# One reciprocal per tile pair, all first-batch gathers on SyncE, and first-batch loads spread over the steps

## The chip, the cores and the metric

The kernel runs on one NeuronCore of a Trainium2 chip. The metric is the device time of one execution in microseconds (us), lower is better. Three runs of the kernel before the change gave 615.82, 616.46 and 617.23 us; the median is 616.46 us. One execution, the one of 617.23 us, was recorded with a hardware profile.

## The reference, cut to what matters

"Talking heads" attention, in which the heads are mixed before and after the softmax, and then a feed-forward network with a squared ReLU:

```python
scores = scale * np.matmul(q, k.transpose(0, 1, 3, 2))      # 8 batches, 12 heads, 448 x 448, head_dim 64
scores = np.einsum('bhij,hg->bgij', scores, w_pre)          # heads mixed
attn = np.exp(scores - max); attn = attn / (sum + 1e-09)    # softmax over j
attn = np.einsum('bhij,hg->bgij', attn, w_post)             # heads mixed again
x = np.matmul(attn, v) -> (3584, 768)
h = np.maximum(x @ w_in, 0.0)                               # w_in 768 x 2048
out = (h * h) @ w_out                                       # w_out 2048 x 768
```

## The kernel before, in words

Each batch is cut into 45 tiles of 10 queries. A tile holds its 10 queries times 12 heads on partitions, so that one matmul with a small block matrix (`pre`) mixes the heads. Two tiles make one step; there are 180 steps `ds` (and two more to drain), 22.5 for each batch. The steps run through these stages:

- `load_qk`, `load_v`, `load_w1`, `load_w2` issue DMAs from GpSimd (POOL). They convert float32 in HBM to bf16 in SBUF. For each batch there are six loads of q and k and three of v; the two weight matrices take eight loads each, once.
- `turn_unit` transposes q and k on TensorE (`tr_ps`), six units for each batch. `TURN` says at which step each unit runs; for batch 1 these are steps 15, 15, 16, 16, 17, 17.
- `score_pair` makes the scores of two heads for a block of 128 queries (`s_ps`); ScalarE (ACT) and VectorE (DVE) each cast one of the two to bf16 into the tile `S` (line 312). A batch has four blocks and there are only two `S` buffers, so the casts of a block wait until every gather from the block two before has landed.
- `gather` copies one tile's rows from `S` to a tile `G` with one DMA of 105 KB from SBUF to SBUF (line 329). There are `AHEAD + 2` = 12 `G` buffers, so a gather can be issued as soon as the `mix` of 12 tiles earlier has been done. At the start tiles 0 to 11 are gathered in one go.
- `mix(k)`, for the two tiles of step `k`, mixes the heads into two PSUM banks (`m_ps`, line 338). For each of them ACT takes the exponential with a row sum (`e_sb`, line 343), DVE the reciprocal of the sum (`rc`, line 345), and POOL scales and shifts (`d`, line 347).
- `unmix(k)`, two steps later (`LAG = 2`), mixes with `w_post` on TensorE (`at_ps`, line 369), and DVE casts into `at` (line 374).
- `av_unit` multiplies with v (`ot_ps`, line 185), ACT writes `xt` (line 196). `ffn1_unit` (`h_ps`, line 234) and `ffn2_unit` (`o_ps`, line 267) are the feed-forward network; they are put into a list of fillers and handed out over the steps by weight.

The order of TensorE and POOL is the order in which the program is written (`manual_schedule`); a planner orders DVE, ACT and SyncE (SP). `at_load(i, f, ...)` puts a load into POOL's order ahead of the work of tile `i`, that is, of step `i // 2`; the list for -1 is issued before step 0. DMAs of SP and ACT share eight completion semaphores in the order of the program, and each DMA waits until the one issued eight before it has landed.

In the kernel before, the gathers of batch 0 go in turn to SP and ACT:

```python
eng = nc.scalar if b == 0 and k % 2 else nc.sync
```

Of the kernel before, what the change touches and what calls it, by code (L numbers as in the profile page):

```python
# [9 lines left out]
F32 = mybir.dt.float32  # L10
ACT = mybir.ActivationFunctionType
# [3 lines left out]
B, H, S, D = 8, 12, 448, 64  # L15
# [18 lines left out]
OFF = 64 - H * (IQ // 2)  # L34
SCALE = 1.0 / 8.0
# [7 lines left out]
def kernel(  # L43
# [11 lines left out]
    nc = tc.nc  # L55
    P = nc.NUM_PARTITIONS
# [4 lines left out]
    work = ctx.enter_context(tc.tile_pool(name="work", bufs=1))  # L61
# [4 lines left out]
    def bank(name, dtype=F32):  # L66
        return psp.tile([P, 512 if dtype == F32 else 1024], dtype, name=name, tag="ps")
# [29 lines left out]
    def stripes(name, p0s):  # L97
        t = consts.tile([P, HQ], F32, name=name)
        for p0, c0 in zip((0, 64), p0s):
# [9 lines left out]
                            in0=stripe_pre[:, :].unsqueeze(2).to_broadcast([P, HQ, H]),  # L109
# [14 lines left out]

    gts = [work.tile([P, S], BF16, name=f"G{x}") for x in range(AHEAD + 2)]
    for t in gts:
        nc.vector.memset(t[0:OFF, :], 0.0)

    attn = [atp.tile([P, R, H, TW], BF16, name=f"at{x}") for x in range(2)]
    for t in attn:  # L130
# [166 lines left out]
    Sb, Gs, dsb = {}, {}, {}  # L297
# [16 lines left out]
    def queries(t, y):  # L314
        return max(0, min(HQ, S - IQ * t - HQ * y))
# [5 lines left out]
    def gather(k):  # L321

        b, t = steps[k]
        blk, tl = divmod(t, TPB)
        n = min(IQ, S - IQ * t)
        x = BLK_OFF[blk] + IQ * tl
        g = gts[k % len(gts)]
        eng = nc.scalar if b == 0 and k % 2 else nc.sync
        eng.dma_start(out=g[OFF:OFF + H * n, :], in_=Sb[(b, blk)][x:x + n, :, :])
        Gs[k] = g  # L330

    def mix(k):
        pss = [bank("m_ps") for _ in range(2)]
        gs = [Gs.pop(2 * k + x) for x in range(2)]
        for y in range(2):
            for x in range(2):
                rows = slice(64 * y, 64 * y + H * queries(steps[2 * k + x][1], y) if y else 64)
                nc.tensor.matmul(pss[y][64 * x:64 * x + 64, 0:S], lhsT=pre[rows, :], rhs=gs[x][rows, :],  # L338
                                 start=True, stop=True)
        for y in range(2):  # L340
            e = work.tile([P, S], F32, name="e_sb", tag="E", bufs=3)
            sm = work.tile([P, 1], F32, name="sm", tag="sm", bufs=4)
            nc.scalar.activation(out=e[:, :], in_=pss[y][:, 0:S], func=ACT.Exp, scale=SCALE, accum_out=sm[:, 0:1])  # L343
            rc = work.tile([P, 1], F32, name="rc", tag="rc", bufs=4)
            nc.vector.reciprocal(out=rc[:, :], in_=sm[:, :])  # L345
            d = dts[(2 * k + y) % ND]
            nc.gpsimd.tensor_scalar(out=d[:, 0:S], in0=e[:, :], scalar1=rc[:, 0:1], scalar2=-1.0 / S,  # L347
                                    op0=ALU.mult, op1=ALU.add)
            dsb[(k, y)] = d

# [43 lines left out]
    with tc.manual_schedule(engines={PE, POOL}):  # L394
# [10 lines left out]
        def at_load(i, f, *args):  # L405
            loads.setdefault(i, []).append(lambda: f(*args))

        for x in range(2):
            at_load(-1, load_w1, x)
        for x in range(3):  # L410
            at_load(-1, load_v, 0, x)
            at_load(44 + x, load_v, 1, x)
        for x in range(2, 8):
            at_load(-1, load_w1, x)
        for x in range(8):
            at_load(18 + 2 * x, load_w2, x)
        for x in range(6):
            at_load(6 + 2 * x, load_qk, 1, x)
            at_load(46 + 2 * x, load_qk, 2, x)
        for b in range(1, B):  # L420
            if b + 2 < B:
# [27 lines left out]
        def gathers_for(ds):  # L449
            while gathered[0] < min(2 * ds + AHEAD + 2, len(steps)):  # L450
                if issued[0] < needs(steps[gathered[0]]):
                    break
                gather(gathered[0])
                gathered[0] += 1
# [6 lines left out]
        for ds in range(nd + LAG):  # L461
# [37 lines left out]
            if now2:  # L499
                mix(ds)  # L500
# [37 lines left out]
```

The softmax here doesn't subtract the row's maximum and nothing guards it: scores larger than these inputs give would overflow.

## Time and profile before

| what | value |
|---|---|
| median of three runs | 616.46 us |
| the profiled execution, its own time | 617.23 us |
| its span, first to last instruction | 615.4 us |
| mean granted TensorE clock | 0.964 |
| busy: PE, DVE, POOL, ACT | 90%, 71%, 65%, 64% |
| gathers from SP / from ACT | 338 / 22 |
| reciprocals on DVE | 360, 154 ns each |

The busy shares are means over stages with different limits. The page cuts the span into 40 slices of 15.4 us each and gives a digit for each engine and slice. TensorE is at 9 in nearly every slice from the 12th on. It is between 4 and 8 in the first eight. The chain of waits names, for each stretch of time, the work that the end of the program hung on. Windows of the span give busy time for each engine in a stretch. A wait is put down to the engine whose semaphore came last.

### The profile page before, as it was taken

The page shows a single profiled execution, that of the slowest core. Times are in us where ns is not written, and L with a number is a line of the kernel's source. Part 1 is how long each engine was busy: PE and PEld are TensorE (multiplying, and loading weights), DVE is VectorE, ACT ScalarE, POOL GpSimd, SP SyncE. Part 2 cuts the span into 40 slices and gives each one's busy share as a digit, 9 for nine tenths or more (in the row PEclk, how much of TensorE's full clock was granted, in tenths as well). Part 3 has the DMA queues.
Part 4 walks back from the last instruction along what each step waited for, and adds up shares of the span by engine and source line. Part 5 has one row for each costly group of instructions (what it writes and reads, how often), then busy time and mean ns, then how long its engine had stood idle before and what let it go on. Part 6 is the DMA issues. An engine that isn't in the chain of part 4 may idle for free.

```text
span 615.4 us, 26843 instructions
## 1 busy us (share of the span) xinstructions
PE 556.6 (90%) x11154; PEld 313.2 (51%) x11154; DVE 434.4 (71%) x1123; ACT 396.1 (64%) x1196; POOL 397.8 (65%) x579
## 2 busy tenths in 40 slices
PE   5456888799799999999999899999999999999997
PEld 3124556554455456545555456545555455555554
DVE  5364999988687778876886768776887787755101
ACT  3364677556678866787578755786678767972320
POOL 7264838657459963898458944798458945892450
PEclk9655999999899999999999999999999999999999
DMA  9989958859645885488545875478543565431102
GB/s 141 227 169 160 199 99 148 149 84 176 140 110 108 131 151 120 100 141 143 124 108 103 131 147 126 91 119 143 137 104 80 101 149 122 87 65 53 40 15 75
DMA packets 90910, 74.10 MB, mean 120 GB/s; under 512 B 6308, under 2 KB 87716, under 8 KB 90788
## 3 DMA queue, kind: packets, MB, share of 16 engines
q1 hardware_dynamic: 48982, 47.20, 32.7%
q0 software_dynamic: 38816, 22.81, 28.6%
q10 hardware_dynamic: 2990, 2.37, 1.3%
q8 instruction: 87, 1.43, 0.9%
q14 instruction: 35, 0.29, 0.1%
HBM read 45.63 MB, written 11.01 MB: 92 GB/s over the span
## 4 chain that ended last, share of the span: by engine, by line
PE 63%; POOL 11%; DVE 11%; DMA 6%; ACT 5%; issue 3%; ACTq 0%; DVEq 0%; POOLq 0%; SPq 0%
PE o_ps L267 22%; PE h_ps L234 17%; PE at_ps L369 7%; PE ot_ps L185 6%; POOL d L347 5%; DVE at L374 5%; DMA G<-S 5%; PE m_ps L338 4%; POOL h L246 3%; PE s_ps L309 3%; PE tr_ps L162 3%; ACT e_sb L343 2%; ACT xt L196 2%; DVE S L312 1%; DVE h L246 1%
## 5 line engine op out<-in xcount | busy, mean ns | idle before, releaser
L347 POOL TENSOR_SCALAR d<-e_sb,rc 128x448 bf16<-128x448 f32 x360 | 228.2, 646 | 173.8 <-DVE rc L345 171.9
L374 DVE CAST at<-at_ps 112x480 bf16<-112x480 f32 x360 | 219.5, 649 | 44.9 <-PE at_ps L369 40.8
L343 ACT ACTIVATE e_sb<-m_ps 128x448 f32<-128x448 f32 x360 | 196.1, 558 | 21.3 <-POOL d L347 9.5
L234 PE MATMUL h_ps<-xt,w 128*128 128x448 bf16 (+2 forms) x960 | 162.9, 316 | 3.8 <-DVE at L374 2.2
L267 PE MATMUL o_ps<-w,h 128*128 128x384 bf16 (+1 forms) x1024 | 163.9, 330 | 0.7 <-ACT xt L196 0.5
L312 ACT CAST S<-s_ps 128x448 bf16<-128x448 f32 x192 | 100.4, 540 | 87.8 <-PE s_ps L309 55.8
L312 DVE CAST S<-s_ps 128x448 bf16<-128x448 f32 x192 | 115.1, 613 | 14.4 <-DMA G<-S 12.3
L267 PEld LDWEIGHTS <-h 128*128 128x128 bf16 (+1 forms) x1024 | 83.3, 101 | 73.4 <-issue 28.4
L246 POOL TENSOR_TENSOR h<-hr 128x448 bf16<-128x448 f32 (+2 forms) x124 | 109.4, 891 | 17.1 <-ACT hr L244 17.1
L234 PEld LDWEIGHTS <-w 128*128 128x128 bf16 x960 | 79.2, 98 | 79.9 <-issue 30.9
L369 PE MATMUL at_ps<-post,d 60*64 60x60 bf16 x5760 | 86.7, 197 | 17.4 <-POOL d L347 8.5
L369 PEld LDWEIGHTS <-d 60*64 60x64 bf16 x5760 | 64.6, 111 | 61.9 <-issue 26.3
L338 PE MATMUL m_ps<-G,pre 64*64 64x448 bf16 x720 | 79.0, 366 | 16.9 <-DMA G<-S 5.1
L244 ACT ACTIVATE hr<-h_ps 128x448 f32<-128x448 f32 (+2 forms) x136 | 68.9, 513 | 27.6 <-PE h_ps L234 11.7
L345 DVE RECIPROCAL rc<-sm 128x1 f32<-128x1 f32 x360 | 50.0, 154 | 41.8 <-ACT e_sb L343 40.0
L343 ACT ACTIVATION_READ_ACCUMULATOR e_sb<-m_ps 128x1 f32 x360 | 78.1, 217 | 0.0
L196 ACT ACTIVATE xt<-ot_ps,bvec 128x160 bf16<-128x160 f32 (+3 forms) x144 | 44.7, 386 | 50.6 <-PE ot_ps L185 39.0
L309 PE MATMUL s_ps<-kT,qT 64*64 64x448 bf16 x768 | 71.7, 369 | 5.1 <-ACT S L312 4.1
L274 DVE COPY osb<-o_ps 128x384 f32<-128x384 f32 x48 | 26.0, 546 | 40.5 <-PE o_ps L267 40.4
L185 PE MATMUL ot_ps<-at,v 112*64 112x160 bf16 (+4 forms) x1152 | 47.3, 234 | 2.8 <-DVE at L374 2.8
L185 PEld LDWEIGHTS <-v 112*64 112x64 bf16 x1152 | 39.8, 112 | 15.8 <-issue 15.3
L338 PEld LDWEIGHTS <-pre 64*64 64x64 bf16 x720 | 27.9, 108 | 35.5 <-issue 26.5
(39 smaller groups left out, 212.5 us busy)
## 6 DMA issues: line engine op xcount, KB each, us to landing
G<-S SPq DMA_DIRECT2D x330, 105.0 KB
kst<-in_k_dram POOLq DMA_DIRECT2D x24, 224.0 KB, 6.1
qst<-in_q_dram POOLq DMA_DIRECT2D x24, 224.0 KB, 6.0
v<-in_v_dram POOLq DMA_DIRECT2D x24, 224.0 KB, 6.5
w<-in_moe_w_in_dram POOLq DMA_DIRECT2D x8, 384.0 KB, 14.0
w<-in_moe_w_out_dram POOLq DMA_DIRECT2D x8, 384.0 KB, 8.7
out_dram<-osb SPq DMA_DIRECT2D x8, 336.0 KB
G<-S ACTq DMA_DIRECT2D x22, 105.0 KB
```

The source lines that it names most:

```text
L185: nc.tensor.matmul(ps[64 * hh:64 * hh + 64, TW * y + c0:TW * y + 2 + n], lhsT=vs[b][0:PR, g, r, :], rhs=at[0:PR, r, g, c0:2 + n], start=(y ...
L234: nc.tensor.matmul(ps[:, 0:n], lhsT=w1[ft // 4][:, c2, ft % 4 * 128:ft % 4 * 128 + 128], rhs=xts[b][:, c2, c0:c1], start=(c2 == 0), stop=( ...
L244: nc.scalar.activation(out=hr[:, 0:n], in_=ps[:, 0:n], func=ACT.Relu)
L246: square.tensor_tensor(out=h2ts[(b, ft)][:, c0:c1], in0=hr[:, 0:n], in1=hr[:, 0:n], op=ALU.mult)
L267: nc.tensor.matmul(dst, lhsT=h2ts[(b, ft)][:, mt * 128:mt * 128 + ROWS[mt]], rhs=w2[ft // 4][:, ft % 4, n2 * 384:(n2 + 1) * 384], start=(f ...
L309: nc.tensor.matmul(pss[hh][z:z + 64, 0:S], lhsT=qTs[b][rs, p, q0:q0 + 64], rhs=kTs[b][rs, p, :], start=True, stop=True)
L312: copy(out=Sb[(b, blk)][:, 2 * p + hh, :], in_=pss[hh][:, 0:S])
L338: nc.tensor.matmul(pss[y][64 * x:64 * x + 64, 0:S], lhsT=pre[rows, :], rhs=gs[x][rows, :], start=True, stop=True)
L343: nc.scalar.activation(out=e[:, :], in_=pss[y][:, 0:S], func=ACT.Exp, scale=SCALE, accum_out=sm[:, 0:1])
L347: nc.gpsimd.tensor_scalar(out=d[:, 0:S], in0=e[:, :], scalar1=rc[:, 0:1], scalar2=-1.0 / S, op0=ALU.mult, op1=ALU.add)
L369: nc.tensor.matmul(us[x][z:z + 64, c:c + HR], lhsT=d[rows, PR * r + z:PR * r + z + 64], rhs=post[rows, :], start=True, stop=True)
L374: nc.vector.tensor_copy(out=dst, in_=src)
```

## The change

It has four parts.

1. In `mix`, the two row sums go to the two columns of one 128x2 tile, one reciprocal takes both, and the two POOL operations come after it. `e_sb` has four buffers in place of three, `sm` and `rc` have three of two columns in place of four of one.
2. All gathers of batch 0 are issued from SP.
3. Loads are moved. The eight loads of `w1` go from the list for -1 to steps 1 to 4, two in each. The six of batch 1's q and k go from steps 3 to 8 to steps 7 to 12. The eight of `w2` go from steps 9 to 16 to steps 14 to 21. The three of batch 0's v stay in the list for -1 and are now alone in it.
4. The twelve memsets of the first 4 rows of the `G` tiles go from DVE to POOL.

```diff
     for t in gts:
-        nc.vector.memset(t[0:OFF, :], 0.0)
+        nc.gpsimd.memset(t[0:OFF, :], 0.0)
...
-        eng = nc.scalar if b == 0 and k % 2 else nc.sync
-        eng.dma_start(out=g[OFF:OFF + H * n, :], in_=Sb[(b, blk)][x:x + n, :, :])
+        nc.sync.dma_start(out=g[OFF:OFF + H * n, :], in_=Sb[(b, blk)][x:x + n, :, :])
...
+        sm = work.tile([P, 2], F32, name="sm", tag="sm", bufs=3)
+        rc = work.tile([P, 2], F32, name="rc", tag="rc", bufs=3)
+        es = []
         for y in range(2):
-            e = work.tile([P, S], F32, name="e_sb", tag="E", bufs=3)
-            sm = work.tile([P, 1], F32, name="sm", tag="sm", bufs=4)
-            nc.scalar.activation(out=e[:, :], in_=pss[y][:, 0:S], func=ACT.Exp, scale=SCALE, accum_out=sm[:, 0:1])
-            rc = work.tile([P, 1], F32, name="rc", tag="rc", bufs=4)
-            nc.vector.reciprocal(out=rc[:, :], in_=sm[:, :])
+            e = work.tile([P, S], F32, name="e_sb", tag="E", bufs=4)
+            nc.scalar.activation(out=e[:, :], in_=pss[y][:, 0:S], func=ACT.Exp, scale=SCALE, accum_out=sm[:, y:y + 1])
+            es.append(e)
+        nc.vector.reciprocal(out=rc[:, :], in_=sm[:, :])
+        for y in range(2):
             d = dts[(2 * k + y) % ND]
-            nc.gpsimd.tensor_scalar(out=d[:, 0:S], in0=e[:, :], scalar1=rc[:, 0:1], scalar2=-1.0 / S,
+            nc.gpsimd.tensor_scalar(out=d[:, 0:S], in0=es[y][:, :], scalar1=rc[:, y:y + 1], scalar2=-1.0 / S,
                                     op0=ALU.mult, op1=ALU.add)
...
-        for x in range(2):
-            at_load(-1, load_w1, x)
+        for x in range(8):
+            at_load(2 + 2 * (x // 2), load_w1, x)
+            at_load(28 + 2 * x, load_w2, x)
         for x in range(3):
             at_load(-1, load_v, 0, x)
             at_load(44 + x, load_v, 1, x)
-        for x in range(2, 8):
-            at_load(-1, load_w1, x)
-        for x in range(8):
-            at_load(18 + 2 * x, load_w2, x)
         for x in range(6):
-            at_load(6 + 2 * x, load_qk, 1, x)
+            at_load(14 + 2 * x, load_qk, 1, x)
             at_load(46 + 2 * x, load_qk, 2, x)
```

## The prediction

> **What bounds the kernel now.** I read the page's slices first, then windows, then the chain of waits of the first 160 us, then the timelines of ACT and POOL there.
>
> ```profile
> PE   5456888799799999999999899999999999999997
> DVE  5364999988687778876886768776887787755101
> PEclk9655999999899999999999999999999999999999
> ```
>
> PE is full from slice 12 on but for single slices, DVE in slices 5 to 8. The first four slices, 61.5 us, have no full engine. The windows (busy us of PE, PEld, DVE, ACT, POOL, then clock, DMA share, GB/s) say the same:
>
> ```profile
> 20.00:40.00 20.00, 7.65 (x164) 3.54 (x168) 6.63 (x19) 9.41 (x28) 6.06 (x10) 0.54 0.99 207
> 40.00:60.00 20.00, 13.04 (x310) 7.80 (x301) 11.51 (x34) 10.70 (x35) 12.06 (x19) 0.52 0.98 159
> 60.00:80.00 20.00, 16.37 (x412) 11.49 (x410) 19.05 (x54) 12.86 (x42) 14.93 (x23) 1.00 1.03 199
> ...
> 400.00:480.00 80.00, 78.47 (x1651) 42.05 (x1643) 61.40 (x155) 60.54 (x184) 60.03 (x87) 1.00 0.60 114
> ```
>
> From 16 to 52 us the DMA engines are full and the rest wait. From 60 to 140 us DVE is (75 of 80 us). From about 160 us it is PE, whose order and work the change leaves alone. So a shift reached at 160 us should arrive at the end. The chain of waits (start, us, what) shows where the first stage goes:
>
> ```profile
> 16.68 7.00 DMA G<-S
> 23.72 0.62 PE m_ps L338 x4
> 24.35 2.26 ACT S L312 x5
> 26.61 0.97 ACT e_sb L343 x4
> 27.58 6.93 DMA G<-S
> ...
> 46.88 3.80 DMA G<-S
> ```
>
> Gathers end three stalls, 17.7 us in all. ACT's timeline has one more loss:
>
> ```profile
> 16.68 7.61 ACTq L329 DMA_DIRECT2D G<-S  x5
> 24.33 2.28 ACT L312 CAST S<-s_ps 128x448 bf16<-128x448 f32 x5 [7.43 <-PE m_ps L338]
> 26.45 0.60 ACT L343 ACTIVATE e_sb<-m_ps 128x448 f32<-128x448 f32 x1
> ```
>
> ACT's fifth gather needs the semaphore of the first, which landed at 22.9. Five casts, then the exponentials of step 0, stand behind it. On POOL, w1 and v are issued during 6.7 to 19.3 us, and steps 3 to 7 go at POOL's pace of 2.0 us (1.26 for two d, 0.73 for a load):
>
> ```profile
> 17.75 1.52 POOL L218 DMA_DIRECT2D w<-in_moe_w_in_dram  x2 [2.06 <-DMA w<-in_moe_w_in_dram]
> ...
> 38.45 1.26 POOL L347 TENSOR_SCALAR d<-e_sb,rc 128x448 bf16<-128x448 f32 x2
> 39.66 0.74 POOL L73 DMA_DIRECT2D qst<-in_q_dram  x1
> 40.44 1.26 POOL L347 TENSOR_SCALAR d<-e_sb,rc 128x448 bf16<-128x448 f32 x2
> ```
>
> **What the skill says.** The Trainium skill, "DMA: Bandwidth & Descriptors", section "Queues, rings and completion order": each DMA engine goes round between the queues that have work, a packet at a time. The trace agrees: at 25 to 38 us, with SP, ACT and POOL queues loaded, a gather took 2.0 us on each of the first two, and a w1 load landed every 3.8 us; at 86 to 98 us, with SP's alone, gathers landed 0.90 us apart, 2.9 us after issue. The same page, "Issuing engines are not separate DMA queues": a second issuer saves only issue time. Here that is 0.77 us (SP) or 0.80 (ACT) for each gather. "TensorE: Matmul & The Clock Gate", "Part 1: The HAM clock gate": idle windows halve TensorE's clock. The trace has it at 0.5 from 21.5 to 59.0 us. I expect that to stay, since steps 0 to 8 remain sparse.
>
> **Part 2 and the w1 move (3), worked together.** ACT loses 22 issues and their waits; SP gets them at 0.87 us apart. The cast that frees the first gather is unmoved at 16.68. Beside the first gathers only v (1.2 us a load) is in flight now, not w1:
>
> - Tiles 0 and 1 land at 19.6 and 20.5 (before: 22.9 and 23.2). mix(0) at 21, not 23.7.
> - Tile 11 is issued at 16.7 + 11 x 0.87 = 26.3 and lands at 29.2 (before 34.1). The casts of block 2 follow at 29.5, not 34.7.
> - POOL now meets two w1 issues (1.52 us) ahead of d in each of steps 1 to 4. With d at 1.26 that is 2.8 us for a step: d(2) 30.9, d(3) 33.7, d(4) 36.5, d(5) 37.8, d(6) 40.2. PE waits for d(k-2) before mix(k), so mix(5) is at 36 and mix(7) at 40.
> - w1's packets come from about 27.8 and meet the gathers, two queues in place of three. From 3.8 us for 3.8 gathers and one w1, and about 2.1 us for a w1 alone (its landings were 1.9 to 2.8 us apart), a gather costs the engines 0.45 us. Packet for packet (120 of a gather, 384 of a w1) a gather then takes 0.45 + 120/384 x 2.1 = 1.1 us; I take 1.2. Tiles 12 to 23 land from 30.1 to 43.3 (tile 23 before: 50.0).
> - Block 3's casts wait for tile 23, so the exponential of step 8 comes at 44.7, not at 52.2: **-7.5 us**. With 1.45 us a gather it is 48.3 (-3.9); with 0.9 the POOL pace holds it at 42.6 (-9.6).
>
> **The later loads (3).** The POOL queue is one line: batch 1's q and k stand behind w1. w1 takes 384/120 x 1.15 = 3.7 us each beside gathers, so it is done at 57; q and k follow at 1.7 (before: eight such landings in 13.3 us), the second at 60.5, the fourth at 64, the sixth at 67.5. The turn units want them at 68.3, 71.4 and 76.7 before, 7.5 earlier now: 60.8, 63.9, 69.2. That is just in time: +0.5, bounds 0 and +7. w2 is wanted from 126.2 (first o_ps), and lands by about 100. But it now lies beside the burst of gathers of tiles 45 to 58 (85.7 to 100 us, 0.9 us apart), whose end the casts of a block at step 24 wait for: 12 gathers at 1.25 in place of 0.92 are 4 us, of which some 3 were free: +1, bounds 0 and +4. POOL's issues cost the same 0.74 as before, and POOL isn't full there (10.7 to 15.7 of 20 us).
>
> **Part 1.** The page's row:
>
> ```profile
> L345 DVE RECIPROCAL rc<-sm 128x1 f32<-128x1 f32 x360 | 50.0, 154 | 41.8 <-ACT e_sb L343 40.0
> ```
>
> A 128x2 reciprocal isn't in the trace. Its nearest rows are a 128x3 DVE operation (159 ns) and a 64x6 one (152), so I take 154: 180 instructions go. In 60 to 140 us, where DVE is full, that is 26 of them; back-to-back pairs start only 0.06 us apart, single ones cost up to 0.15: **-2 us** (26 x 0.08), bounds 0 and -3.8. Later, DVE is off the path: 0. The wait that it adds: d of the first tile now waits for the second exponential. Put step by step against the trace, the second reciprocal ended after that d's start in 131 of 180 steps, by 0.15 us on average over all, since DVE is usually late for both. PE's first use of d came typically 2 to 3 us later. Delay beyond that slack sums to 0.8 us over steps 10 to 179: **+0.8**, bounds 0 and +2. In steps 0 to 9 it is within the times above. On DVE the casts of `at` stand behind this reciprocal, by at most one exponential's 0.53. The fourth e buffer frees ACT of "e_sb waits for d" (9.5 us, 18 times): 0 to -1, I take 0.
>
> **Part 4.** POOL's 12 memsets of 448 columns: its 128x1 took 0.1, its 128x128 0.23, so about 0.55 by a line, 6.6 us at most. They end at 13, before mix(0) at 21, and hold back v (issued at about 13, used at 54.8 before). DVE loses 2.89 us ahead of its wait for k. Cost 0, hidden behind the first loads (to 12.8).
>
> **Sum.** -7.5 + 0.5 + 1 - 2 + 0.8 = -7.2 against the profiled 617.23, which lies 0.8 above the median of 616.46. The same shift from the median gives **609.5 us**.
>
> **The rivals.**
> - *The POOL queue is late* (slower, 23%). If a gather beside w1 takes 1.45 us, the early gain is 3.9, a w1 takes 4.6, and w1 ends at 65. Batch 1's loads then land at 68.4 to 75 where 64 to 70 is wanted: +6. w2 slides to 103, and all of the burst goes at 1.5: +4 or more, with the merge at its +2. -3.9 + 6 + 4 + 2 - 2 = +6, so 622.5. It decides when w1's last load lands after some 62 us. For it: DMA is full for 60 us already. Against: most of w1 falls where gathers wait for PE.
> - *Hidden anyway* (same, 7%). As above with no burst loss: the turn units set the pace of steps 15 to 18 and eat the gain: 616.5.
> - *More* (8%). Gathers hardly feel w1: -9.6, and -3.8 of reciprocals: 603.
> - Forecast (62%): 605 to 614.
>
> Chances: faster by over 0.2% (1.2 us, about what a measurement tells from no change) 0.70, within 0.07, slower 0.23. The range 603 to 619 leaves out about 0.15 above and 0.04 below.
>
> **What would show it.** No G issue on ACT and its five casts at once behind the others, ending before 20 us; mix(0) near 21; block 2's casts near 29.5; the exponential of step 8 near 44.7; w1 landed by 57 and no PE wait for q or k at the first turn units; DVE still full for 60 us after that. Wrong: step 8 later than 49, a `tr_ps` wait on DMA around 62 to 70, or a shift at step 10 that is gone at step 45.

## The result, and the profile after

The changed kernel takes **625.02 us** (median of four runs, 624.03 to 626.83), the kernel before 616.14 beside it: a ratio of 1.0150, 95% interval 1.0116 to 1.0185. It is slower by 8.9 us where 609.5 was forecast. Its profiled execution took 626.83 us, 9.6 more than that of before, with a span of 625.0 and a mean TensorE clock of 0.958.

The same three rows of the page's slices, now of the changed kernel (its slices are 15.6 us long):

```profile
PE   4535886799799999999999989999999999999997
DVE  3444997698588668866776767866886687655101
PEclk9755999899899999999999999999999999999999
```

DVE's third and fourth digits fall from 6 and 4 to 4 and 4, and its seventh and eighth from 9 and 9 to 7 and 6: those are the two places where time was lost, at 31 to 62 us and at 94 to 125 us. From there on the rows look as before. The windows of the changed kernel, with the columns of those of before, put numbers to it:

```profile
20.00:40.00 20.00, 6.20 (x108) 2.57 (x108) 4.62 (x12) 5.94 (x19) 6.77 (x11) 0.58 0.84 154
40.00:60.00 20.00, 10.65 (x248) 5.80 (x250) 11.90 (x28) 9.52 (x30) 13.24 (x21) 0.50 1.01 185
60.00:80.00 20.00, 16.81 (x438) 12.41 (x434) 16.30 (x42) 13.19 (x45) 14.87 (x23) 0.90 0.84 142
...
100.00:120.00 20.00, 11.91 (x304) 9.02 (x302) 11.43 (x30) 9.14 (x33) 12.48 (x19) 0.83 0.96 167
...
400.00:480.00 80.00, 78.19 (x1610) 42.44 (x1608) 58.44 (x126) 58.77 (x179) 59.29 (x85) 1.00 0.63 120
```

The kernel before had at 100 to 120 us:

```profile
100.00:120.00 20.00, 16.98 (x453) 12.41 (x456) 18.99 (x56) 13.44 (x47) 15.73 (x26) 1.00 1.04 166
```

At 20 to 40 us DVE runs 12 instructions in place of 19 and ACT 19 in place of 28; at 100 to 120 us PE works 11.9 us where it had worked 17.0. The chain of waits (start, us, what) names both losses:

```profile
28.86 8.52 DMA G<-S
...
37.42 0.21 DVE S L312
...
44.98 3.85 DMA G<-S
...
100.45 10.61 DMA G<-S
...
111.97 2.77 PE ot_ps L185 x48
```

Gathers end both stalls: 8.5 us of the chain in the first place, 10.6 us in the second (before, this second place had no DMA in its chain at all). The start of the exponential of a step's first tile, read in both traces, follows the shift through the program:

| step | before | after | shift |
|---|---|---|---|
| 0 | 26.45 | 22.59 | -3.9 |
| 2 | 35.50 | 27.03 | -8.5 |
| 3 | 36.96 | 38.67 | +1.7 |
| 8 | 52.19 | 55.93 | +3.7 |
| 23 | 98.07 | 101.91 | +3.8 |
| 24 | 101.31 | 111.81 | +10.5 |
| 40 | 149.49 | 157.38 | +7.9 |
| 45 | 166.31 | 174.91 | +8.6 |
| 179 | 560.02 | 569.37 | +9.3 |

What the gathers do at step 3 stands in the timelines of ACT, DVE and POOL (start, us from first start to last end, what, and in brackets the wait ahead of it):

```profile
15.43 4.47 ACT L312 CAST S<-s_ps 128x448 bf16<-128x448 f32 x10
22.59 0.54 ACT L344 ACTIVATE e_sb<-m_ps 128x448 f32<-128x448 f32 x1 [2.70 <-PE m_ps L337]
...
37.42 1.16 DVE L312 CAST S<-s_ps 128x448 bf16<-128x448 f32 x2 [10.29 <-DMA G<-S]
38.49 0.15 DVE L346 RECIPROCAL rc<-sm 128x2 f32<-128x2 f32 x1
...
38.75 1.25 POOL L349 TENSOR_SCALAR d<-e_sb,rc 128x448 bf16<-128x448 f32 x2 [9.15 <-DVE rc L346]
```

ACT's ten casts end before 20 us and step 0 starts at 22.6, as forecast. Then DVE stands for 10.3 us in front of the cast of block 2, which needs tile 11 to have landed. The exponentials of step 2 had been done by 28.2, but their reciprocal is behind that cast in DVE's order, and d of step 2 behind the reciprocal: POOL stands for 9.2 us. All that steps 0 to 2 had gained is lost there, and 1.7 us more.

At step 24 it is ACT's cast of a block that stands, until 111.06, for tile 56, issued at 100.45:

```profile
111.38 0.53 ACT L312 CAST S<-s_ps 128x448 bf16<-128x448 f32 x1 [6.58 <-DMA G<-S]
```

Read from the trace, gather by gather. A gather has landed here with the last of its 120 packets, counted in the order of their starts. The trace doesn't say which packet belongs to which gather, so this holds only while the DMA engines keep step; a waiting cast sees the semaphore, which is complete when the last part is there.

| | before | after |
|---|---|---|
| first gather issued | 16.68 | 17.50 |
| first w1 issued / last landed | 6.7 / 40.5 | 25.3 / 57.2 |
| tiles 0 to 7, landings apart | 1.0 (two each 2.0) | 0.9 |
| tiles 9 to 13, landings apart | 1.3 | 1.6 |
| tile 11 landed / its semaphore complete | 34.05 / 34.51 | 35.48 / 37.30 |
| w2 issued / landed | 54.3 to 75.5 / 61.5 to 84.3 | 73.6 to 98.0 / 81.2 to 105.9 |
| tiles 45 to 57, landings apart | 0.96 | 1.33 |
| tiles 45 to 56, semaphores complete, apart | 0.94 | 1.59 |
| tile 56 issued / landed / semaphore complete | 95.8 / 98.6 / 99.6 | 100.5 / 107.1 / 111.1 |

### The profile page after: what moved, and what is told of

Same layout as the page of the kernel before. It is cut to its first block, busy times and chain, and to the rows that moved or that the text cites. A ratio compares the mean times of both kernels' runs of the same rounds, so it can differ in the third digit from the quotient of the medians.

```text
span 625.0 us, 26804 instructions
## 1 busy us (share of the span) xinstructions
PE 554.3 (89%) x11154; PEld 313.4 (50%) x11154; DVE 416.2 (67%) x931; ACT 392.4 (63%) x1196; POOL 402.1 (64%) x591
## 3 DMA queue, kind: packets, MB, share of 16 engines
q0 software_dynamic: 38816, 22.81, 28.8%
## 4 chain that ended last, share of the span: by engine, by line
PE 60%; POOL 15%; DVE 7%; DMA 7%; issue 6%; ACT 3%; SPq 2%; ACTq 0%; DVEq 0%; POOLq 0%
PE o_ps L267 22%; PE h_ps L234 14%; POOL d L349 7%; PE at_ps L371 7%; PE ot_ps L185 6%; DMA G<-S 6%; POOL h L246 5%; PE m_ps L337 4%; DVE at L376 4%; PE s_ps L309 3%; PE tr_ps L162 3%; SPq L328 2%; POOL kst L73 1%; ACT xt L196 1%; DMA qst<-in_q_dram 1%
## 5 line engine op out<-in xcount | busy, mean ns | idle before, releaser
L267 PE MATMUL o_ps<-w,h 128*128 128x384 bf16 (+1 forms) x1024 | 162.2, 328 | 0.6 <-ACT xt L196 0.5
L312 ACT CAST S<-s_ps 128x448 bf16<-128x448 f32 x192 | 99.6, 541 | 97.0 <-PE s_ps L309 63.2
L371 PE MATMUL at_ps<-post,d 60*64 60x60 bf16 x5760 | 88.9, 197 | 23.7 <-POOL d L349 12.2
L371 PEld LDWEIGHTS <-d 60*64 60x64 bf16 x5760 | 65.4, 111 | 69.8 <-POOL d L349 30.2
L337 PE MATMUL m_ps<-G,pre 64*64 64x448 bf16 x720 | 77.8, 366 | 20.5 <-ACT S L312 9.0
L309 PE MATMUL s_ps<-kT,qT 64*64 64x448 bf16 x768 | 69.8, 373 | 0.4
L185 PE MATMUL ot_ps<-at,v 112*64 112x160 bf16 (+4 forms) x1152 | 48.6, 238 | 8.4 <-ACT S L312 5.6
L346 DVE RECIPROCAL rc<-sm 128x2 f32<-128x2 f32 x180 | 29.0, 161 | 38.6 <-ACT e_sb L344 17.8
## 6 DMA issues: line engine op xcount, KB each, us to landing
w<-in_moe_w_in_dram POOLq DMA_DIRECT2D x8, 384.0 KB, 10.5
```

What stands on the lines that cost most here:

```text
L185: nc.tensor.matmul(ps[64 * hh:64 * hh + 64, TW * y + c0:TW * y + 2 + n], lhsT=vs[b][0:PR, g, r, :], rhs=at[0:PR, r, g, c0:2 + n], start=(y ...
L267: nc.tensor.matmul(dst, lhsT=h2ts[(b, ft)][:, mt * 128:mt * 128 + ROWS[mt]], rhs=w2[ft // 4][:, ft % 4, n2 * 384:(n2 + 1) * 384], start=(f ...
L309: nc.tensor.matmul(pss[hh][z:z + 64, 0:S], lhsT=qTs[b][rs, p, q0:q0 + 64], rhs=kTs[b][rs, p, :], start=True, stop=True)
L312: copy(out=Sb[(b, blk)][:, 2 * p + hh, :], in_=pss[hh][:, 0:S])
L371: nc.tensor.matmul(us[x][z:z + 64, c:c + HR], lhsT=d[rows, PR * r + z:PR * r + z + 64], rhs=post[rows, :], start=True, stop=True)
```

## The experiments

The theory after the result had two losses: w1 catches the first burst of gathers (tiles 0 to 11), and w2 the burst of tiles 45 to 58. The rivals were the POOL queue (q and k of batch 1 late), the reciprocal, and the memsets. "Step n" below is the shift of that step's first exponential against the profiled execution of before. One profiled execution can lie some us from its kernel's median, so both are given. The ratio is always to the kernel before, with its 95% interval.

**One part alone, from the kernel before.** Four kernels; the first takes only the new `mix`:

```diff
-            rc = work.tile([P, 1], F32, name="rc", tag="rc", bufs=4)
-            nc.vector.reciprocal(out=rc[:, :], in_=sm[:, :])
...
+        rc = work.tile([P, 2], F32, name="rc", tag="rc", bufs=3)
...
+        nc.vector.reciprocal(out=rc[:, :], in_=sm[:, :])
```

> The kernel before with the merged reciprocal alone. Theory A: nothing to lose, DVE has 26 instructions less while it is full: 614 to 616.5. Theory C: most of the loss: 620 to 625.

Measured 615.0 us, ratio 0.9994 (0.9974 to 1.0014). Step 8 at -1.5, step 40 at -4.4, step 179 at -3.9 in a profile of 613.6 us. The reciprocal isn't the loss.

```diff
-        nc.vector.memset(t[0:OFF, :], 0.0)
+        nc.gpsimd.memset(t[0:OFF, :], 0.0)
```

> The kernel before with the twelve memsets on POOL alone. If POOL's 5 us of memsets hold back nothing that is awaited: 615 to 617. They also hold back w1 by 5 us, which then lies more beside the first gathers: up to +3, 619. If they account for the whole +5.8: 621 to 622.

Measured 615.28, ratio 0.9981 (0.9962 to 1.0000); step 8 at +0.15. With both of these in one kernel:

```diff
+        nc.vector.reciprocal(out=rc[:, :], in_=sm[:, :])
...
+        nc.gpsimd.memset(t[0:OFF, :], 0.0)
```

> The kernel before with the merged reciprocal and the memsets on POOL, all loads and both issuers as before. Alone each gave about -1. If both are real and independent: 613 to 615. If they hold back w1 and d in the first block together: 616 to 618.

Measured 617.5, ratio 1.0019 (1.0001 to 1.0037), step 40 at -3.9. By these medians parts 1 and 4 move the time by 0.2% at most, either way; the intervals reach to 0.4%.

```diff
-        eng = nc.scalar if b == 0 and k % 2 else nc.sync
-        eng.dma_start(
+        nc.sync.dma_start(
```

> The kernel before with all gathers of batch 0 on SP alone, nothing else. If the single queue is what costs in the first block (the other runs give +5.8 for it and the memsets together): step 8 later by 4 to 5, 620 to 622. If it is the memsets on POOL: 615 to 617.

Measured 617.41, ratio 1.0017 (0.9998 to 1.0036): a miss, as 620 to 622 had been expected of the single queue. Step 2 is 4.5 us late and steps 8 to 40 are 2.4 late, but step 41, which waits for gathers in both kernels, gives it all back. This kernel has w1 beside the gathers from the start, and tiles 1 to 8 land 1.57 us apart, as tiles 9 to 13 do in the changed kernel.

**The loads alone.** Only the loads of part 3 are moved:

```diff
+            at_load(2 + 2 * (x // 2), load_w1, x)
+            at_load(28 + 2 * x, load_w2, x)
...
+            at_load(14 + 2 * x, load_qk, 1, x)
```

> The kernel before with the moved loads alone (w1 at steps 1 to 4, q and k of batch 1 at 7 to 12, w2 at 14 to 21); gathers of batch 0 in turn from SP and ACT, two reciprocals. Theory A: with two issuers the first twelve gathers are issued by 22 us, ahead of w1's first packets at about 28, so the early loss turns into a gain of 3 to 7 us at step 8, but the stall at step 24 (+6 to +7) stays: 616 to 620. Theory B: no loss: 610 to 616. If w1's place alone makes the early loss, whoever issues: 624 to 626.

Measured 619.42, ratio 1.0061 (1.0031 to 1.0091). The early gain is there (step 8 at -4.0, step 22 at -3.3) and the second loss too (step 24 at +1.3). Its profiled execution, 615.3 us, is among its fastest. Then w2 alone in the kernel before:

```diff
-            at_load(18 + 2 * x, load_w2, x)
+            at_load(28 + 2 * x, load_w2, x)
```

> The kernel before with the w2 loads alone moved to steps 14 to 21. Theory A: step 8 as before; at step 24 a stall of 4 to 7 us: 619 to 623. If the stall at step 24 needs the late q and k as well (one POOL queue, in which w2 stands behind them): 616 to 617.

Measured 620.65, ratio 1.0077 (1.0042 to 1.0113): step 22 at -1.7, step 24 at +2.1, step 179 at +3.4. Late w2 alone makes the kernel slower. And w1 at steps 1 to 4 with the new `mix` alone, gathers still on two queues:

```diff
-            at_load(-1, load_w1, x)
+            at_load(2 + 2 * (x // 2), load_w1, x)
```

> The kernel before with the merged reciprocal and with w1 at steps 1 to 4; gathers of batch 0 in turn from SP and ACT, q and k of batch 1 at steps 3 to 8, w2 at steps 9 to 16, memsets on DVE. Theory A with two issuers: step 8 is 4 us earlier than before as with the moved loads alone, nothing stalls at step 24, and DVE's stage gives 2 to 3 us: 609 to 612. If POOL, which now has w1 and q/k loads ahead of d in steps 3 and 4, sets the pace: 613 to 616.

Measured 618.12, ratio 1.0036 (1.0014 to 1.0058), above both ranges that were expected. Step 2 at -5.9, step 7 at +2.4 (POOL has w1's issues and q's and k's in the same steps), step 8 at -1.7. Its profiled execution took 614.2, 3.9 below its median, so that the shifts say less here than the ratio. Against e3 (0.9994), from which it differs in w1's place alone, it is the slower one: by the medians, w1's move gained nothing even with two gather queues.

**One part undone, from the changed kernel.** First w2 alone goes back to where it was:

```diff
-            at_load(28 + 2 * x, load_w2, x)
+            at_load(18 + 2 * x, load_w2, x)
```

> The changed kernel with one edit: the eight w2 loads back at steps 9 to 16. Theory A (collision: weight loads that run beside a burst of gathers slow the gathers; w2 at steps 14 to 21 meets the burst of tiles 45 to 58): the stall at step 24 goes, 625 less 6 to 7, so 618 to 619; the early loss at step 8 (+3.7) stays. Theory B (one queue for all gathers is what costs, whatever loads are in flight): little changes, 623 to 625. Theory C (the merged reciprocal costs, as d of the first tile waits longer): 624 to 625.

Measured 621.99, ratio 1.0129 (1.0078 to 1.0180). The stall at step 24 is gone (+3.7 there), but the time misses the expected 618 to 619: steps 14 to 16 are up to 4.5 us late for q and k, which now stand behind w2 in POOL's queue. All loads back:

```diff
+            at_load(-1, load_w1, x)
+            at_load(18 + 2 * x, load_w2, x)
+            at_load(6 + 2 * x, load_qk, 1, x)
```

> The changed kernel with all loads back where they were before; what is left is one reciprocal, all gathers on SP, and the memsets on POOL. Theory A: no collision at step 24; in the first block w1 is in flight from the start beside a single gather queue, at about 1.6 us a gather, so tile 11 lands at 37 to 39 and step 8 is 2 to 4 us later than before: 617 to 620. Theory B: the whole loss stays: 622 to 625. Theory C: 622 to 625.

Measured 620.81, ratio 1.0102 (1.0060 to 1.0143): step 7 at +8.1, step 24 at +3.8, and just above the expected range. With w1 in flight from the start, the single queue's first twelve gathers need until 40.8 us. This kernel differs from e11 (1.0019) in the issuers alone. So the single queue cost 0.8% with all loads in their old places too, and step 41 gave back little of it, unlike in e7.

**Two kernels that made a third loss.** In the changed kernel, w2 back at steps 9 to 16 and w1 two steps later:

```diff
-            at_load(2 + 2 * (x // 2), load_w1, x)
-            at_load(28 + 2 * x, load_w2, x)
+            at_load(6 + 2 * (x // 2), load_w1, x)
+            at_load(18 + 2 * x, load_w2, x)
```

> The changed kernel with w2 back at steps 9 to 16 and w1 two steps later, at steps 3 to 6: its first packets then follow the first twelve gathers, which still go from SP alone. If the early loss is w1 catching that burst: tile 11 lands at 29 to 31 in place of 35, the exponential of step 3 comes at 31 to 33 in place of 37 to 39, step 8 is 2 to 5 us earlier than before, and the time is 612 to 617, against 622 with w1 at steps 1 to 4. If the single queue costs by itself: 620 to 623.

Measured 625.58, ratio 1.0145 (1.0104 to 1.0186), above both expected ranges. Tile 11 lands at 30.1 and step 3 comes at 32.3, 6.4 us sooner than in the changed kernel: that collision is what w1's place decides. But step 17 is at +9.5. The chain of waits of this kernel:

```profile
46.71 20.89 DMA qst<-in_q_dram
...
67.89 17.94 DMA qst<-in_q_dram
...
85.88 0.96 PE tr_ps L162 x16
```

A load of q takes 21 us from issue to landing, the last one 18, since w1 and w2 are ahead of and between them in POOL's queue, and the turn units wait. This is the prediction's slower rival, in a kernel made for another purpose. The other one is the kernel before with the new `mix`, w1 at steps 1 to 4, q and k at 7 to 12, and w2 left at 9 to 16:

```diff
+            at_load(2 + 2 * (x // 2), load_w1, x)
             at_load(18 + 2 * x, load_w2, x)
+            at_load(14 + 2 * x, load_qk, 1, x)
```

> The kernel before with the merged reciprocal, w1 at steps 1 to 4, q and k of batch 1 at steps 7 to 12; two issuers, w2 at steps 9 to 16, memsets on DVE. With the first burst out before w1 and no q/k loads in the way at steps 3 to 6, step 8 should be 4 us earlier than before and stay so, and nothing stalls at step 24: 610 to 613. If w2 and q/k on one queue at steps 9 to 12 collide with the turn units or the gathers: 616 to 619.

Measured 621.95, ratio 1.0087 (1.0057 to 1.0117), again above both: step 8 at -4.6, step 17 at +4.1, the last of q and k landed at 80.5. The same rival.

**Each loss taken away alone, then both.** Two issuers again in the changed kernel, all else of it kept:

```diff
-        nc.sync.dma_start(
+        eng = nc.scalar if b == 0 and k % 2 else nc.sync
+        eng.dma_start(
```

> The changed kernel with one edit: gathers of batch 0 in turn from SP and ACT again. If the single queue let w1 catch the first burst: tile 11 lands at 27 to 29, step 8 is about 4 us earlier than before in place of 3.7 later, the stall at step 24 stays at 4 to 6: 616 to 619. If the issuers don't matter: 624 to 625.

Measured 619.14, ratio 1.0050 (1.0030 to 1.0071). The timelines of its DVE and ACT at the two places:

```profile
30.55 1.15 DVE L312 CAST S<-s_ps 128x448 bf16<-128x448 f32 x2
...
100.99 0.53 ACT L312 CAST S<-s_ps 128x448 bf16<-128x448 f32 x1 [4.99 <-DMA G<-S]
```

Block 2's cast comes at 30.6 with no wait, in place of 37.4 after 10.3 us; the stall at step 24 is still there. Two things help here: the first burst's gathers land 0.7 to 0.8 us apart from two queues, and step 0 comes late again (26.1 us), so that POOL issues w1 only at 28.8, when tile 11 has landed (28.6). Step 8 is at -4.1. This run doesn't tell the two apart. Then w1 two steps later and nothing else, on the single queue:

```diff
-            at_load(2 + 2 * (x // 2), load_w1, x)
+            at_load(6 + 2 * (x // 2), load_w1, x)
```

> The changed kernel with its w1 loads two steps later (steps 3 to 6), all else as in the change, so that q and k of batch 1 stand behind w1 alone. Theory of two collisions: the first burst of gathers is left alone, tile 11 lands by 31, the exponential of step 3 comes at about 32 (changed kernel 38.7) and of step 8 at 51 (55.9); the stall of 5 to 7 us at step 24 stays, as w2 is where it was. End 3 to 5 us below the changed kernel: 620 to 622. Rival, the POOL queue: w1 ends later, q and k of batch 1 land after 72 and the turn units of steps 15 to 17 wait, so that step 17 is no better than in the changed kernel: 625.

Measured 624.02, ratio 1.0132 (1.0087 to 1.0178). Half a miss. The traced steps came as the theory had them: step 3 at 32.4, step 8 at 51.0 (-1.1), and the profiled execution, 623.46, is 3.4 below the changed kernel's. The median is only 1.0 below, where 3 to 5 was expected, and the two intervals overlap. So in the traces w1's place alone takes away 4.9 of the 7.9 us that the second issuer takes away at step 8, but the times don't show this gain. The stall at step 24 stayed (6.8 us), and step 17 lost 1.3 us to q and k, which landed up to 76.9 (74.6 in the changed kernel). Then w2 in pairs at steps 13 to 16, and nothing else:

```diff
-            at_load(28 + 2 * x, load_w2, x)
+            at_load(26 + 2 * (x // 2), load_w2, x)
```

> The changed kernel with w2 issued two in a step at steps 13 to 16, behind q and k of batch 1 and ahead of the gathers of tiles 45 to 58. Theory: the stall at step 24 falls from 6.7 us to under 2, q and k are not late, and from step 24 on the kernel is +3 to +5 against before in place of +8 to +10: 619 to 621. Rival: w2 has too little time from there, its last load still lands beside the burst (after 95 us), and the stall is 4 us or more: 623 to 625.

Measured 621.13, ratio 1.0071 (1.0053 to 1.0090), at the edge of what the theory had. ACT's cast at the second place has no wait left, and the shift goes from +2.5 at step 23 to +2.6 at step 24:

```profile
103.46 0.53 ACT L312 CAST S<-s_ps 128x448 bf16<-128x448 f32 x1
```

Last, both: two issuers, and w2 in pairs.

```diff
+        eng = nc.scalar if b == 0 and k % 2 else nc.sync
...
+            at_load(26 + 2 * (x // 2), load_w2, x)
```

> The changed kernel with both collisions taken away: first batch's gathers from two issuers again, and w2 two in a step at steps 13 to 16. Theory: step 8 at -4, step 24 at -3 against before, and the end at -3 to -5: 611 to 613, faster than both kernels. Rival: what is gained by step 24 is given back where PE is full (the first d of a pair waits for the second exponential, the clock dips), and the end is within 1.5 us of before: 615 to 617.

Measured **614.7 us**, ratio 0.9978 (0.9954 to 1.0002). That is below the changed kernel beyond doubt, but not told from the kernel before (nor from e3 and e8), where 611 to 613 was expected. The four kernels make a square, as ratios to before:

| | w2 late (steps 14 to 21) | w2 in pairs (13 to 16) |
|---|---|---|
| gathers from SP alone | 1.0150 (the change) | 1.0071 |
| gathers from SP and ACT | 1.0050 | 0.9978 |

Each edit is worth about the same with and without the other: 0.72% to 0.79% for w2's place, 0.93% to 1.00% for the second issuer. As each ratio is known to 0.2 to 0.35%, this fits two independent losses, which together make up the distance to before; it does not exclude that a part of them is shared.

Where e15's gain went: it is at -4.2 on step 24 and at -7.0 on step 40, then -5.4 on step 41, -4.7 on step 45, -3.6 on step 108 and -2.0 on step 179. At step 41 PE waits for a block's casts, and these for gathers. PE's timeline there, in the kernel with both avoided and in the kernel before:

```profile
152.49 0.63 PE L372 MATMUL at_ps<-post,d 60*64 60x60 bf16 x30 [5.01 <-ACT S L312]
```

```profile
157.86 0.57 PE L369 MATMUL at_ps<-post,d 60*64 60x60 bf16 x30 [3.20 <-ACT S L312]
```

The kernel that comes 7.0 us sooner waits 1.8 us longer. The gather that ends the wait is the last one of batch 1, tile 89: issued at 143.9 and complete at 151.8 in e15, at 149.2 and 157.2 before, 8 us each time. The v loads of batch 2, issued at 140.8 to 145.1 in e15 and at 147.8 to 152.3 before, are in flight beside it. That looks like a third collision, which the kernel before has too; no run moved these loads. Around its end TensorE's clock is at half for 6.8 us in e15 (from 150.8) and for 3.4 us before (from 158.0). The rest is lost in small pieces where PE is full. Part of it is the merged reciprocal's (e3 loses 1.2 us between steps 41 and 107 too); 1.1 us at step 160 has no cause that these traces show.

## Why the prediction was wrong, by its own steps

- **What bounds the kernel**: right. Both losses lie in the stage that the windows had shown to be bound by DMA and by DVE, and a shift of +8.7 at step 41 arrived as +9.6 at the end. For a gain the premise "should arrive at the end" was too strong, as e15 shows. The prediction's own sign of being wrong, step 8 later than 49, is what came (55.9).
- **Tiles 0 and 1, mix(0) at 21, no gather on ACT, its casts before 20 us**: right but for a us: 20.6 and 21.4 for 19.6 and 20.5, and mix(0) at 21.2.
- **Tile 11 lands at 29.2: the step that failed first.** Its parts: the first gather was issued at 17.50, not at 16.68 (+0.8, the first q and k landed later), and the next ones 0.91 apart and not 0.87 (+0.4). That alone makes 30.6, 27.54 and the 3.05 us that tiles 0 to 7 took. The text said itself that w1's packets come from 27.8, and charged them only to tiles 12 to 23. Tiles 9 to 11 were still under way then, and took 1.6 us and more each. The semaphore of tile 11 was complete at 37.3: 8.1 us late. e9 and e13, in which w1 comes later, have step 3 at 32.3 and 32.4.
- **A gather beside w1, 1.2 us with 1.45 as its bound**: the term that was mis-sized, 1.6 measured. It was worked out as packet for packet between two queues, 120 to 384, as if both kinds lay on the same DMA engines. The traces say otherwise: each gather has ten 4-byte packets (220 for ACT's 22 before) and its semaphore ten increments from DMAs, each load has sixteen such packets (1428 for 89). Read as one for each engine in use, a gather has 12 packets on each of ten engines and a w1 load 24 on each of sixteen. Turn for turn, one w1 load then lets 2 gathers of one queue pass, or 4 of two queues. Measured: 1.9 for each w1 load of 3.0 us after, and 3.8 for each of 3.8 us before. So the Trainium skill, "DMA: Bandwidth & Descriptors", section "Queues, rings and completion order", gives the right form (on each engine, each queue with work has its turn), and the traces agree once a transfer is counted on the engines that it uses. As an estimate with the prediction's own 0.45 and 2.1 us, a gather beside w1 is 0.45 + 12/24 x 2.1 = 1.5 us. Moving all gathers to one queue halves their turns beside w1. The prediction said "two queues in place of three" and took the gathers to be helped by that.
- **The same page, "Issuing engines are not separate DMA queues"**, on which the prediction took a second issuer to save issue time alone: the runs here don't agree. With w1 beside them, gathers landed 1.0 us apart from two queues (before) and 1.57 from one (e7), where SP would have issued one each 0.8 to 0.9 us; tile 11's semaphore was complete at 34.5 and at 39.1. The measurement decides. That the change took 619.1 us with two issuers and 625.0 without doesn't settle this point, as there the burst was out before w1 came.
- **The reciprocal on the path**: missed. d(2) was put at 30.9, bound by POOL's w1 issues. No step asked what stands ahead of the reciprocal in DVE's order: the cast of block 2, so the late gather held d(2) until 38.8 as well.
- **-7.5 for the early part** was +3.7 at step 8: 11.2 us of the miss of 16.8 between the profiled executions (forecast -7.2, measured +9.6). The sum's last line is also off by 0.2 us: 616.46 less 7.2 is 609.3, not 609.5.
- **q and k of batch 1, +0.5**: right in the shift. w1 was done at 57.2 (forecast 57), but by luck: a load took 3.0 us beside gathers and not 3.7, and POOL, held up by d(2), issued the last four only from 40 us on. q and k landed at 62.3, 65.4 and 74.6 for 60.5, 64 and 67.5, beside turn units that were later too; the shift is +3.7 at step 10 and +3.6 at step 22.
- **w2 beside the burst, +1 with +4 as its bound**: mis-sized, +6.7, beyond the bound. Counted by packets the landings were 1.33 us apart for a forecast of 1.25: nearly right. But the cast waits for the last part of tile 56, and the semaphores of tiles 45 to 56 were complete 1.59 us apart, 0.94 before: over eleven gathers 7.2 us. Tile 56 took 10.6 us from issue to semaphore, not 3.8; its ten increments came from 104.9 to 111.1 us, those of before within 1.5 us. The sum had priced the mean rate of all packets, and a step that waits for a gather pays for its slowest part. Why one part trailed stays open. e14 and e15 take the stall away with w2's place alone.
- **The reciprocal, -2**: 161 ns for the 128x2 form (154 taken). The page's row after:

```profile
L346 DVE RECIPROCAL rc<-sm 128x2 f32<-128x2 f32 x180 | 29.0, 161 | 38.6 <-ACT e_sb L344 17.8
```

  In steps 24 to 40 the shift falls by 2.6 in the changed kernel and by 2.8 in e3, and by 2.2 to 2.9 in all kernels with the merged one; with two reciprocals it goes from a fall of 1.3 (e4) to a rise of 1.1 (e6). The size is about right. **The merge, +0.8**: between steps 45 and 179 the changed kernel loses 0.7 us. That includes a gain of 1.5 that isn't its own, as the kernel before had a stretch of half clock near 352 us that this execution lacks. So some 2.2 us, just over its bound of 2. For the whole kernel, e3's ratio of 0.9994 (0.9974 to 1.0014) doesn't tell the forecast of -1.2 us from nothing.
- **Part 4, 0**: right. POOL's timeline shows its price, below the 6.6 us of the bound; v was issued at 11.6 to 13.8:

```profile
6.17 5.00 POOL L127 MEMSET G<- 4x448 bf16 x12
```

- **The rival that came nearest in time, "the POOL queue is late" (622.5, slower)**, wasn't what happened: w1 ended at 57.2, before its point of 62. It had the second loss in its sum (+4) and the rate of 1.45. Its own mechanism showed in e1, e9 and e10.

## What to carry to other kernels

When a load is moved behind a burst of small transfers, charge it to those that are still under way at that moment, and ask when the last part of the one transfer that a step waits for is there, not only for the mean rate of all. Before transfers are put on one queue, count on how many DMA engines each transfer lies and how many turns each queue has there beside the others: fewer queues for one kind of work means a smaller share for it, not less traffic. And follow every engine's written order past the waiting instruction: a cast that waits for a gather held a reciprocal, and so another engine, that had nothing to do with that gather.

## What the hardware showed that was not expected

- The parts of one gather can land far apart. The ten increments of tile 56's semaphore came over 6.2 us in the changed kernel (104.86 to 111.06, w2 in flight) and over 1.5 us before (98.07 to 99.56). Those of tile 11 came over 2.3 us (35.01 to 37.30) and 0.3 us (34.23 to 34.51), with w1 in flight in both kernels, so that a load beside a gather is not by itself the reason.
- Gathers beside w1 loads landed 1.57 us apart from one queue (e7, tiles 1 to 8) and 1.0 us apart from two (before).
- The runs of one kernel spread with the granted clock: e12's 20 runs took 615.5 to 624.8 us at mean clocks between 0.956 and 0.964, with a correlation of -0.79. One dip to half clock, of 3.4 us, falls on step 107 in seven of the seventeen traces (before, e1, e2, e6, e7, e8, e15) and is missing in the others, the changed kernel among them. The windows of e15 and of before, each with the clock as third from last, show it; PE was busy for 2.63 of 4 us just ahead of it.

```profile
344.00:348.00 4.00, 2.63 (x68) 1.38 (x72) 2.08 (x5) 2.03 (x6) 3.96 (x6) 1.00 0.83 149
348.00:352.00 4.00, 3.81 (x28) 1.57 (x14) 2.41 (x5) 2.03 (x6) 3.92 (x7) 0.59 0.84 103
```

```profile
348.00:352.00 4.00, 2.63 (x54) 1.29 (x51) 2.29 (x6) 2.41 (x7) 3.96 (x7) 1.00 0.88 149
352.00:356.00 4.00, 3.81 (x15) 1.76 (x13) 2.05 (x6) 1.96 (x6) 3.92 (x8) 0.57 0.71 93
```

  By the shifts, which fall by 1.5 us at steps 108 to 109 in the changed kernel and in e3 against before, one such dip cost 1.5 us. So a difference of one or two us between two profiled executions says nothing without the medians.
